# Value packs with zero weights put into a planned TensorE queue of an attention kernel

## The chip, the cores and the metric

The kernel runs on one core of one Trainium2 chip. The metric is device microseconds of one execution, as the median of several. A profile of one more execution gives the rows below; times in them are microseconds from the start of the span unless marked ns. The engines are TensorE (PE, and PEld for its weight loads), VectorE (DVE), ScalarE (ACT), GpSimd (POOL) and SyncE (SP).

## The reference

One input x (1 × 2048 × 512, bf16) goes through two branches with 32 heads of width 16; a sigmoid gate mixes the results per token.

```python
g = sigmoid((x * gate_w).sum(-1, keepdims=True))
# A: softmax attention
scores = einsum("bhqd,bhkd->bhqk", q, k) * 16 ** -0.5
o = einsum("bhqk,bhkd->bhqd", softmax(scores), v)   # then @ A_wo
# B: linear attention with feature maps
phi = concat([softmax(p), softmax(-p)]), p = einsum("bhsd,hdf->bhsf", q or k, w_phi)
o = (phi_q @ (phi_k.T v)) / (phi_q @ phi_k.sum() + 1e-6)   # then @ B_wo
return g * a + (1 - g) * b
```

Branch A has 32 × 2048 × 2048 scores, and an exponential of each.

## The kernel before

**Units and packs.** Branch A is cut into units: the scores of one head, 128 keys (on the partitions) and 512 queries. Four units with the same keys and queries, of four heads, make a pack; there are 512 packs, 16 to a group (16 blocks of 128 keys, `kt` = 0 to 15), and 2048 units.

**Scores.** `_scores` (L663) issues one matmul per unit, which uses 32 of the array's 128 rows; `_qk` issues those of a group of 3 or of 2 units in turn, at different row positions, so that they run beside each other. A group's scores lie in 3 or 2 of a ring of 5 banks of the accumulator memory, so a score group has to wait for the exponential two groups earlier.

**Exponentials.** `_exp` (L702) takes one ACTIVATE on ACT per group, 1536 or 1024 columns: 762 of them for 1905 units. The other 143 units have their exponential made on DVE from integer operations (L597 to L615, from a score matmul named `vqk`).

**Values.** `_pv` queues for each pack one TensorE operation, `_values` (L738): four matmuls (three where DVE makes the fourth unit), each with 128 rows and 32 of the 128 columns of the array, at four column positions side by side; they add into one bank, `ot`, over the 16 key blocks. A unit made on DVE comes as one such matmul by itself (`pvx`). After the last key block `_norm` divides by the sum (L752 to L763).

**The rest.** The projections (`_proj`, L500; values L541), the transposes of x (L478), all of branch B (L836 to L946) and the output projections (L942, L962) are matmuls on the whole 128 × 128 array. They are spread over the span and lie in TensorE's queue between score groups and value packs.

**What sets the order.** Nothing is ordered by hand. `Plan.op` notes each operation with a cost in planned microseconds, its dependencies and a priority; `Plan.order` then plays all engines through, picks at each step the operation that can start first (ties within 0.02 by priority; score groups have priority −1000), and so fixes each engine's queue. `Plan.emit` writes the queues out with the waits on semaphores. Each engine then works its queue strictly in that order. On TensorE a change of `kind` (row for scores, col for values, full) adds `SWITCH` = 0.12 in the plan, and the costs of matmuls in the plan are 0.23 for a score group or a value pack.

Of the kernel before, what the change touches and what calls it, by code (L numbers as in the profile page):

```python
# [10 lines left out]
P = 128  # L11
# [6 lines left out]
F32, BF16 = dt.float32, dt.bfloat16  # L18
# [21 lines left out]
class Op:  # L40
    def __init__(self, eng, fn, cost, name, prio, rel, kind, lat):
        self.eng, self.fn, self.cost, self.name = eng, fn, cost, name
        self.prio, self.rel, self.kind, self.lat = prio, rel, kind, lat
        self.deps = []
        self.users = []
        self.left = 0
        self.need = False
        self.acquire = None
        self.release = None
        self.sem = None  # L50
        self.start = self.end = None
        self.on_commit = None


class Plan:
# [3 lines left out]
    ENGS = ("PE", "ACT", "DVE", "POOL", "SP")  # L59
    LAT = {"PE": 0.20, "ACT": 0.16, "DVE": 0.08, "POOL": 0.12, "SP": 2.2}  # L60
    SWITCH = 0.12

    def __init__(self):
        self.ops = []
# [1 line left out]
        self.free_banks = []  # L66

    def op(self, eng, fn, cost, reads=(), writes=(), deps=(), name="", prio=0.0, rel=-99, kind="full",
           acquire=None, release=None, lat=None):
        o = Op(eng, fn, cost, name, prio, rel, kind, self.LAT[eng] if lat is None else lat)  # L70
        found = {}
        for b in reads:
            for w in b.writers:
                found[id(w)] = w
        for b in writes:
            for w in b.readers or b.writers:
                found[id(w)] = w
            if b.readers:
                for w in b.writers:
                    found[id(w)] = w  # L80
        for d in deps:
            if d is not None:
                found[id(d)] = d
        found.pop(id(o), None)
        o.deps = list(found.values())
        for b in reads:
            b.readers.append(o)
        for b in writes:
            b.writers, b.readers = [o], []
        o.acquire, o.release = acquire, release  # L90
        self.ops.append(o)
        return o

    def order(self):
        avail = {e: [] for e in self.ENGS}
        for o in self.ops:
            o.left = len(o.deps)
            for d in o.deps:
                d.users.append(o)
        for o in self.ops:  # L100
            if not o.left:
                avail[o.eng].append(o)
        free = dict.fromkeys(self.ENGS, 0.0)
        last_kind = None
        queues = {e: [] for e in self.ENGS}
        left = len(self.ops)
        seq = {id(o): i for i, o in enumerate(self.ops)}
        while left:
            best = None
            for e in self.ENGS:  # L110
                for o in avail[e]:
                    if o.rel > self.now:
                        continue
                    t = free[e]
                    for d in o.deps:
                        r = d.end + (d.lat if d.eng != e or e != "PE" else 0.0)
                        if r > t:
                            t = r
                    if o.acquire is not None:
                        if not self.free_banks:  # L120
                            continue
                        r = min(b[1] for b in self.free_banks)
                        if r > t:
                            t = r
                    o.ready = t
                    key = (t, o.prio, seq[id(o)])
                    if best is None or key < best[0]:
                        best = (key, e)
            if best is None:
                low = min((o.rel for e in self.ENGS for o in avail[e] if o.rel > self.now), default=None)  # L130
                assert low is not None, [(o.name, o.eng) for e in self.ENGS for o in avail[e]][:9]
                self.now = low
                continue
            t0, e = best[0][0], best[1]
            pick = None
            for o in avail[e]:
                if o.rel > self.now or (o.acquire is not None and not self.free_banks):
                    continue
                if o.ready <= t0 + 0.02:
                    key = (o.prio, seq[id(o)])  # L140
                    if pick is None or key < pick[0]:
                        pick = (key, o)
            o = pick[1]
            avail[e].remove(o)
            t = max(o.ready, free[e])
            cost = o.cost
            if e == "PE" and o.kind != last_kind:
                cost += self.SWITCH
                last_kind = o.kind
            o.start, o.end = t, t + cost  # L150
            free[e] = o.end
            queues[e].append(o)
            left -= 1
            if o.acquire is not None:
                k = min(range(len(self.free_banks)), key=lambda i: self.free_banks[i][1])
                bank, _, ops = self.free_banks.pop(k)
                o.acquire.bank = bank
                o.deps.extend(ops)
            if o.release is not None:
                self.free_banks.append((o.release.bank, o.end + o.lat, [o]))  # L160
            if o.on_commit:
                o.on_commit(o)
            for u in o.users:
                u.left -= 1
                if not u.left:
                    avail[u.eng].append(u)
        self.queues = queues
        return queues
# [83 lines left out]
class _Kernel:  # L252
# [33 lines left out]
    def _memory(self, ctx):  # L286
# [15 lines left out]
        self.mask = sb("mask", [P, 2], F32)  # L302
        self.bm = sb("bm", [P, 4], F32)
        self.gw = sb("gw", [P, 4], BF16)
        self.gexp = sb("gexp", [P, 2, NT], F32)
        self.gcol = sb("gcol", [P, 2, NT], F32)
        xn_at = at[0]
# [82 lines left out]
    def _consts(self):  # L390
        op = self.plan.op
        B = Buf
# [16 lines left out]
            self.V[:, :, :, 0:136].rearrange("p t c (h v) -> p (t c) h v", v=17)[:, :, :, 16:17], 1.0), 1.0, prio=-70)  # L409
        self.o_vpad = op("POOL", lambda e: e.memset(self.V[:, :, :, 136:], 0.0), 0.5, prio=-69)  # L410
        self.o_vbones = op("POOL", lambda e: e.memset(self.VB[:, :, :, 64:65], 1.0), 0.3, prio=-20)
        self.o_ot = op("DVE", lambda e: e.memset(self.ot, 1.0), 0.6, prio=-60)
        self.b_wphi0 = B()
        z = op("POOL", lambda e: e.memset(self.wphi[:], 0.0), 0.6, prio=-30)
# [165 lines left out]
    def _vector_units(self, g):  # L580
# [11 lines left out]
        for j, u in enumerate(units):  # L592
            job = Job()
            m = op("PE", lambda e, u=u, job=job: self._scores(e, u, self._bank(job)), 0.23,
                   reads=self._score_bufs([u]), name="vqk", prio=due + 2 * j, rel=due + 2 * j - 3, kind="row",
                   acquire=job)
            parts.append(op("DVE", lambda e, j=j, job=job: e.tensor_scalar(  # L597
                vt[:, j, :], self._bank(job), SCALE * LOG2E * 2.0 ** 23, 127.0 * 2 ** 23 + C0 * 2 ** 16,
                op0=ALU.mult, op1=ALU.add), self.c_dve(512), deps=[m] + self.b_vt.readers, name="v_bits",
                prio=due + 2 * j - 40, release=job))  # L600
# [73 lines left out]
    def _qk(self, a, b):  # L674
        plan, NR = self.plan, self.NRING
        units = self.mine[a:b]

        def run(e):
            for k, u in enumerate(units):
                ins = self._scores(e, u, self.ps[:, (a + k) % NR, :])  # L680
            return ins
        k = len(self.qks)
        for x in range(a, b):
            self.in_group[x] = k
        o = plan.op("PE", run, 0.23, reads=self._score_bufs(units), name=f"qk{k}", prio=-1000, kind="row",
                    deps=[self.exps[k - 2]] if k >= 2 else
                    [self.early[x] for x in range(a, b) if x in self.early])

        def commit(_):
            plan.now = max(plan.now, (units[-1] + 1) // 4)  # L690
        o.on_commit = commit
        self.qks.append(o)
# [16 lines left out]
    def _pv(self, p):  # L709
# [9 lines left out]
        if kt == NT - 1:  # L719
            deps += self.late  # L720
            self.late = []
        o = self.plan.op("PE", lambda e: self._values(e, g8, kt, src), 0.23, deps=deps, name=f"pv{p}", prio=p + 2.5,
                         kind="col")
        self.pvs.append(o)
        for u in range(4 * p, 4 * p + 4):
            if u not in self.place:
                tile, made, buf = self.theirs[u]
                x = self.plan.op("PE", lambda e, u=u, tile=tile: self._values(e, g8, kt, {u % 4: tile}), 0.1,
                                 deps=[o] + self.b_V[g8 // 2][kt // 4].writers, reads=[buf], name="pvx", prio=p + 2.6,
                                 kind="col")  # L730
                self.late.append(x)
        if kt == NT - 1:
            self._norm_a(g, o)
# [1 line left out]
    def _values(self, e, g8, kt, src):  # L735
        for i, tile in src.items():
            v0 = 17 * (2 * i + g8 % 2)
            ins = e.matmul(self.ot[32 * i:32 * i + 32, :], self.V[:, kt, g8 // 2, v0:v0 + 32], tile,  # L738
                           start=(kt == 0), stop=(kt == self.NT - 1), tile_position=(0, 32 * i), skip_group_check=True)
        return ins  # L740

    def _norm_a(self, g, last):
        qc, g8 = divmod(g, 8)
# [282 lines left out]
```

## Time and profile before

| | us |
|---|---|
| median of 3 runs | 1002.81 |
| lowest and highest | 1001.78, 1014.02 |
| the profiled execution's own time | 1007.54 |
| its span, from the first to the last instruction | 1005.8 |
| granted TensorE clock, mean over the span | 0.681 of full speed |

The span is what the rows of the profile describe. The granted clock takes two values in it, 1.00 (2.4 GHz) and 0.50 (1.2 GHz). A row of the waits names who waited, at which line, for whom, the total, how many times and the longest. A row of the timeline merges like instructions that follow each other: its start, the time from the first's start to the last's end, engine, line, what is written from what, and the count; a bracket gives idle time of the engine before it and what ended that.

### The profile page before, as it was taken

The page shows a single profiled execution, that of the slowest core. Times are in us where ns is not written, and L with a number is a line of the kernel's source. Part 1 is how long each engine was busy: PE and PEld are TensorE (multiplying, and loading weights), DVE is VectorE, ACT ScalarE, POOL GpSimd, SP SyncE. Part 2 cuts the span into 40 slices and gives each one's busy share as a digit, 9 for nine tenths or more (in the row PEclk, how much of TensorE's full clock was granted, in tenths as well). Part 3 has the DMA queues.
Part 4 walks back from the last instruction along what each step waited for, and adds up shares of the span by engine and source line. Part 5 has one row for each costly group of instructions (what it writes and reads, how often), then busy time and mean ns, then how long its engine had stood idle before and what let it go on. Part 6 is the DMA issues. An engine that isn't in the chain of part 4 may idle for free.

```text
span 1005.8 us, 12680 instructions
## 1 busy us (share of the span) xinstructions
PE 877.1 (87%) x5344; PEld 229.0 (23%) x5344; DVE 735.7 (73%) x1020; ACT 909.6 (90%) x796; POOL 5.2 (1%) x11
## 2 busy tenths in 40 slices
PE   6989898998789879988889998888988898899886
PEld 3333322222121212211112122221221221221111
DVE  3576777658776787766777878888787888787741
ACT  2998999889997999998998989999899999999995
POOL 2000000000000000000000000000000000000000
PEclk9986987559665775855557559675676756855666
DMA  6100000000000000000000000000000000000000
GB/s 210 43 2 1 1 1 2 1 1 1 1 1 1 1 1 1 1 1 1 1 1 1 1 1 11 11 1 1 1 16 6 1 1 1 17 6 1 1 1 22
DMA packets 9737, 9.22 MB, mean 9 GB/s; under 512 B 2512, under 2 KB 9168, under 8 KB 9680
## 3 DMA queue, kind: packets, MB, share of 16 engines
q1 hardware_dynamic: 8624, 7.36, 2.4%
q10 hardware_dynamic: 1056, 1.05, 0.3%
q8 instruction: 42, 0.69, 0.3%
q14 instruction: 15, 0.12, 0.0%
HBM read 6.31 MB, written 2.10 MB: 8 GB/s over the span
## 4 chain that ended last, share of the span: by engine, by line
ACT 52%; PE 43%; DVE 2%; DMA 1%; issue 1%; SPq 0%; DVEq 0%
ACT ET L702 51%; PE ps L663 19%; PE ps L738 11%; PE ps L500 6%; PE ps L942 2%; PE ps L541 1%; ACT bexp L854 1%; PE ps L930 1%; PE ps L836 1%; DVE vt L597 1%; DMA xn<-in_A_x_dram 1%; PE ps L913 1%; PE ps L962 1%; PE ps L876 0%; DVE bsum L856 0%
## 5 line engine op out<-in xcount | busy, mean ns | idle before, releaser
L702 ACT ACTIVATE ET<-ps 128x1536 bf16<-128x1536 f32 x762 | 881.9, 1274 | 82.0 <-PE ps L663 77.9
L663 PE MATMUL ps<-qT,kT 32*128 32x512 bf16 x2048 | 432.5, 521 | 103.1 <-ACT ET L702 98.7
L738 PE MATMUL ps<-ET,V 128*32 128x512 bf16 x1905 | 272.8, 524 | 0.6 <-DVE T L752 0.6
L663 PEld LDWEIGHTS ps<-qT,kT 32*128 32x128 bf16 x2048 | 81.8, 96 | 431.5 <-ACT ET L702 333.9
L597 DVE TENSOR_SCALAR vt<-ps 128x512 uint32<-128x512 f32 x143 | 97.9, 688 | 83.1 <-PE ps L663 82.2
L738 PEld LDWEIGHTS ps<-ET,V 128*32 128x32 bf16 x1905 | 54.2, 99 | 184.7 <-issue 174.5
L615 DVE SCALAR_TENSOR_TENSOR vu<-vt,vu 128x2560 int16<-128x2560 uint32 (+1 forms) x31 | 80.7, 2602 | 0.2
L752 DVE STREAM_TRANSPOSE T<-ps 128x512 f32<-128x512 f32 x64 | 45.3, 709 | 43.0 <-PE ps L738 42.3
L738 PE MATMUL ps<-vu,V 128*32 128x512 bf16 x143 | 75.6, 529 | 0.0
L500 PE MATMUL ps<-xT,WB 128*128 128x512 bf16 x128 | 44.2, 447 | 1.4 <-DVE qT L525 0.7
L500 PE MATMUL ps<-xT,WA 128*128 128x512 bf16 x128 | 44.5, 456 | 0.5 <-DVE vt L597 0.3
L856 DVE TENSOR_REDUCE bsum<-bexp 128x64 f32<-128x1024 bf16 x32 | 38.7, 1211 | 6.2 <-ACT bexp L854 6.0
L605 DVE TENSOR_SCALAR vf<-vt 128x2560 int16<-128x2560 int16 (+1 forms) x31 | 42.7, 1378 | 0.4
L613 DVE TENSOR_TENSOR vu<-vu,vf 128x2560 f16<-128x2560 f16 (+1 forms) x31 | 42.7, 1379 | 0.3
L609 DVE TENSOR_TENSOR vu<-vu,vf 128x2560 f16<-128x2560 f16 (+1 forms) x31 | 42.7, 1378 | 0.3
L861 DVE TENSOR_TENSOR phi<-bexp,brec 128x1024 bf16<-128x1024 bf16 x32 | 39.0, 1218 | 0.3
L854 ACT ACTIVATE bexp<-bsub 128x1024 bf16<-128x1024 bf16 x32 | 34.5, 1080 | 0.0
L815 DVE CAST qkB<-ps 128x512 bf16<-128x512 f32 x32 | 22.0, 687 | 16.6 <-PE ps L500 16.3
L525 DVE TENSOR_SCALAR qT<-ps,mask 128x512 bf16<-128x512 f32 x32 | 23.6, 738 | 12.2 <-PE ps L500 12.0
L842 DVE TENSOR_REDUCE bmx<-ps 128x32 f32<-128x512 f32 x32 | 21.9, 684 | 10.1 <-PE ps L836 10.0
L500 PE MATMUL ps<-WB,xT 128*128 128x512 bf16 x64 | 27.0, 525 | 2.1 <-DVE vt L597 1.8
L541 PE MATMUL ps<-WA,xT 128*128 128x128 bf16 x256 | 26.5, 260 | 0.4 <-DVE vt L597 0.4
(62 smaller groups left out, 508.5 us busy)
## 6 DMA issues: line engine op xcount, KB each, us to landing
xn<-in_A_x_dram SPq DMA_DIRECT2D x4, 512.0 KB, 8.9
out_dram<-outt SPq DMA_DIRECT2D x16, 128.0 KB, 1.7
WB<-in_B_wqkv_dram SPq DMA_DIRECT2D x1, 1536.0 KB, 9.7
WA<-in_A_wqkv_dram ACTq DMA_DIRECT2D x2, 512.0 KB, 7.2
WA<-in_A_wqkv_dram SPq DMA_DIRECT2D x1, 512.0 KB, 9.2
wphi<-in_B_w_phi_dram SPq DMA_DIRECT2D x32, 0.5 KB, 3.4
WoB<-in_B_wo_dram SPq DMA_DIRECT2D x32, 16.0 KB, 1.8
WoA<-in_A_wo_dram SPq DMA_DIRECT2D x1, 512.0 KB, 3.7
```

Of the source, the lines that this page charges most:

```text
L500: ins = e.matmul(self._bank(job)[:, 0:n], lhs(c), rhs(c), start=(c == 0), stop=(c == 3))
L597: parts.append(op("DVE", lambda e, j=j, job=job: e.tensor_scalar(vt[:, j, :], self._bank(job), SCALE * LOG2E * 2.0 ** 23, 127.0 * 2 ** 23 ...
L605: op("DVE", lambda e: e.tensor_scalar(flat(vf), bits, 127, None, op0=ALU.bitwise_and), 0.16 + n * 0.00053, reads=[self.b_vt], writes=[self ...
L609: op("DVE", lambda e: e.tensor_tensor(flat(vu), flat(vu), flat(vf), ALU.mult), 0.16 + n * 0.00053, reads=[self.b_vf, b_vu], writes=[b_vu], ...
L613: op("DVE", lambda e: e.tensor_tensor(flat(vu), flat(vu), flat(vf), ALU.mult), 0.16 + n * 0.00053, reads=[self.b_vf, b_vu], writes=[b_vu], ...
L615: o = op("DVE", lambda e: e.scalar_tensor_tensor(out=flat(vu).bitcast(I16), in0=flat(vt), scalar=2.0 ** -16, in1=flat(vu), op0=ALU.mult, o ...
L663: return e.matmul(out, self.kT[32 * i:32 * i + 32, cp, kt * TOK:(kt + 1) * TOK], self.qT[32 * i:32 * i + 32, s, :], start=True, stop=True, ...
L702: o = plan.op("ACT", lambda e: e.activation(self.ET[:, a % NS:a % NS + n, :], self.ps[:, a % NR:a % NR + n, :], ACT.Exp, scale=SCALE), sel ...
L738: ins = e.matmul(self.ot[32 * i:32 * i + 32, :], self.V[:, kt, g8 // 2, v0:v0 + 32], tile, start=(kt == 0), stop=(kt == self.NT - 1), tile ...
L752: t1 = op("DVE", lambda e: e.transpose(T1.rearrange("p b s -> p (b s)"), src()), 0.74, deps=[last], writes=[b_T1], name="n_t1", prio=due - ...
L854: op("ACT", lambda e: e.activation(ex.rearrange("p s f -> p (s f)"), sub.rearrange("p s f -> p (s f)"), ACT.Exp), self.c_act(1024) + 0.1, ...
L861: op("DVE", lambda e: e.tensor_tensor(self.phi[:, slot].rearrange("p h (s f) -> p s h f", s=2), ex.rearrange("p s (h f) -> p s h f", f=DH) ...
```

## The change

The planner gets a measure of how much of the array the planned TensorE operations use. Each operation has `array`, its cost where nothing else is said, 0.0533 for each unit's matmul in a score group, a value pack, `vqk` or `pvx`. When `order` has picked a TensorE operation, it adds up `array` of the TensorE operations that were planned to start in the last `SPAN` = 3.0 us. A value pack (all but the one with `kt` = 0 of each group) may carry up to two fill packs; as long as the sum is under `SHARE` × `SPAN` = 1.8 us, one is added, for 0.2133 planned us. A fill pack is four matmuls with the shape, column positions and moving tiles of a value pack, whose weights are a tile of zeros, adding into the same bank `ot`; it adds 0 to the result. It stands behind the wait of its value pack and ahead of the pack's own matmuls. The tile of zeros, 128 × 32, is set once on POOL.

```diff
+        self.array = 0.0
+        self.filler = 0
+        self.filled = 0
...
+    SPAN, SHARE, FILL = 3.0, 0.6, 0.2133
...
+        o.array = cost if array is None else array
...
+            if e == "PE":
+                recent = [r for r in recent if r[0] > t - self.SPAN]
+                recent.append((t, o.array))
+                while o.filler > o.filled and sum(r[1] for r in recent) < self.SHARE * self.SPAN:
+                    o.filled += 1
+                    cost += self.FILL
+                    recent.append((t, self.FILL))
             o.start, o.end = t, t + cost
...
+        self.zero = sb("zero", [P, 32], BF16)
...
+        self.b_zero = B()
+        op("POOL", lambda e: e.memset(self.zero[:], 0.0), 0.1, writes=[self.b_zero], prio=-75)
...
-        o = self.plan.op("PE", lambda e: self._values(e, g8, kt, src), 0.23, deps=deps, name=f"pv{p}", prio=p + 2.5,
-                         kind="col")
+        def run(e):
+            for _ in range(o.filled):
+                self._fill(e, src)
+            return self._values(e, g8, kt, src)
+        o = self.plan.op("PE", run, 0.23, reads=[self.b_zero], deps=deps, name=f"pv{p}", prio=p + 2.5, kind="col",
+                         array=0.0533 * len(src))
+        o.filler = 2 if kt else 0
...
+    def _fill(self, e, src):
+
+        for i in range(4):
+            tile = src.get(i, src[0])
+            e.matmul(self.ot[32 * i:32 * i + 32, :], self.zero[:], tile, start=False, stop=False,
+                     tile_position=(0, 32 * i), skip_group_check=True)
```

In the queue as it is built 565 fill packs (2260 matmuls) stand ahead of 326 of the 512 value packs: two ahead of 239, one ahead of 87.

TensorE's queue at a place with little besides scores and values, near 0.50 ms of the span; L663 (after: L679) are the score matmuls, L738 (L760) the value matmuls, `vu` a tile that DVE made, L913 (L942) a transpose of branch B, `zero` the new tile. Before:

```order
L913 MATMUL ps<-iden,phi 128x128 x8
L663 MATMUL ps<-qT,kT 128x512 x3
L738 MATMUL ps<-ET,V 32x512 x4
L663 MATMUL ps<-qT,kT 128x512 x2
L738 MATMUL ps<-ET,V 32x512 x3
L738 MATMUL ps<-vu,V 32x512
L663 MATMUL ps<-qT,kT 128x512 x3
L738 MATMUL ps<-ET,V 32x512 x4
L663 MATMUL ps<-qT,kT 128x512 x6
L738 MATMUL ps<-ET,V 32x512 x4
```

With the change, at the same place:

```order
L942 MATMUL ps<-iden,phi 128x128 x8
L679 MATMUL ps<-qT,kT 128x512 x3
L760 MATMUL ps<-ET,V 32x512 x4
L679 MATMUL ps<-qT,kT 128x512 x6
L768 MATMUL ps<-ET,zero 32x512 x8
L760 MATMUL ps<-ET,V 32x512 x4
L679 MATMUL ps<-qT,kT 128x512 x2
L768 MATMUL ps<-ET,zero 32x512 x8
L760 MATMUL ps<-ET,V 32x512 x3
L760 MATMUL ps<-vu,V 32x512
L679 MATMUL ps<-qT,kT 128x512 x6
L768 MATMUL ps<-ET,zero 32x512 x8
```

Behind the transposes the first value pack has none, and then two fill packs (x8) stand ahead of each value pack; the score group that follows a pack comes behind all three.

TensorE's queue at a place with projections (L500, after L516), near 0.65 ms. Before:

```order
L500 MATMUL ps<-xT,WB 128x512 x2
L663 MATMUL ps<-qT,kT 128x512 x3
L738 MATMUL ps<-ET,V 32x512 x4
L663 MATMUL ps<-qT,kT 128x512
L500 MATMUL ps<-xT,WA 128x512 x4
L663 MATMUL ps<-qT,kT 128x512 x5
L738 MATMUL ps<-ET,V 32x512 x4
L500 MATMUL ps<-xT,WB 128x512 x2
```

With the change:

```order
L679 MATMUL ps<-qT,kT 128x512 x4
L760 MATMUL ps<-ET,V 32x512 x4
L679 MATMUL ps<-qT,kT 128x512
L516 MATMUL ps<-xT,WB 128x512 x4
L679 MATMUL ps<-qT,kT 128x512 x2
L516 MATMUL ps<-xT,WA 128x512 x2
L679 MATMUL ps<-qT,kT 128x512 x3
L768 MATMUL ps<-ET,zero 32x512 x4
L760 MATMUL ps<-ET,V 32x512 x4
L679 MATMUL ps<-qT,kT 128x512 x2
```

Here the value packs among the projections carry no fill pack or one; the projections keep their rough place, in other portions.

## Rows read from the trace of the kernel before

**Rows 1.** The page: busy time by engine, and the granted clock in 40 slices.

```profile
PE 877.1 (87%) x5344; PEld 229.0 (23%) x5344; DVE 735.7 (73%) x1020; ACT 909.6 (90%) x796; POOL 5.2 (1%) x11
...
PEclk9986987559665775855557559675676756855666
```

**Rows 2.** The waits, two rows.

```profile
PE ps L663 <- ACT ET L702: 98.7, 215, 1.5
...
ACT ET L702 <- PE ps L663: 77.9, 95, 16.3
```

**Rows 3.** Timeline of ACT: the first exponentials, some in the middle, the last.

```profile
19.42 5.97 ACT L702 ACTIVATE ET<-ps 128x1536 bf16<-128x1536 f32 x5 [16.29 <-PE ps L663]
...
439.73 4.62 ACT L702 ACTIVATE ET<-ps 128x1536 bf16<-128x1536 f32 x4
445.06 19.94 ACT L702 ACTIVATE ET<-ps 128x1536 bf16<-128x1536 f32 x17 [0.72 <-PE ps L663]
464.85 1.09 ACT L854 ACTIVATE bexp<-bsub 128x1024 bf16<-128x1024 bf16 x1
465.80 4.66 ACT L702 ACTIVATE ET<-ps 128x1024 bf16<-128x1024 f32 x4
...
527.38 2.39 ACT L702 ACTIVATE ET<-ps 128x1536 bf16<-128x1536 f32 x2
...
993.61 1.02 ACT L702 ACTIVATE ET<-ps 128x1024 bf16<-128x1024 f32 x1 [0.92 <-PE ps L663]
```

**Rows 4.** Windows: PE, PEld, DVE, ACT, POOL busy (x); one at 2.4 GHz, sum of 21.

```profile
19.42:69.67 50.25, 44.56 (x370) 16.24 (x368) 31.16 (x46) 50.23 (x45) 0.00 (x0) 1.00 0.10 22
...
sum 336.97, PE 281.33 PEld 88.66 DVE 279.60 ACT 328.98 POOL 0.00; mean PE 13.40 PEld 4.22 DVE 13.31 ACT 15.67 POOL 0.00
```

**Rows 5.** Windows: one of the 21 stretches at 1.2 GHz, and their sum.

```profile
428.07:533.88 105.81, 91.08 (x495) 19.85 (x495) 72.77 (x85) 99.09 (x88) 0.00 (x0) 0.50 0.00 1
...
sum 638.24, PE 581.96 PEld 132.06 DVE 443.84 ACT 579.37 POOL 0.00; mean PE 27.71 PEld 6.29 DVE 21.14 ACT 27.59 POOL 0.00
```

**Rows 6.** Timeline at 1.2 GHz: projections ahead of a score group.

```profile
652.25 1.89 PE L500 MATMUL ps<-xT,WA 128*128 128x512 bf16 x4
...
654.71 2.37 ACT L702 ACTIVATE ET<-ps 128x1024 bf16<-128x1024 f32 x2 [1.98 <-PE ps L663]
```

**Rows 7.** Groups by line and form: the two forms of the exponential.

```profile
L702 ACT ACTIVATE ET<-ps 128x1536 bf16<-128x1536 f32 x381 | 566.6, 1487 | 66.6 <-PE ps L663 64.0
L702 ACT ACTIVATE ET<-ps 128x1024 bf16<-128x1024 f32 x381 | 404.2, 1061 | 15.5 <-PE ps L663 13.9
```

**Rows 8.** Windows, L500 alone: sum at 2.4 GHz, then at 1.2 GHz.

```profile
sum 336.97, PE 59.47 PEld 13.14; mean PE 2.83 PEld 0.63
sum 638.24, PE 51.03 PEld 8.88; mean PE 2.43 PEld 0.42
```

**Rows 9.** Timeline of PE in a stretch at 2.4 GHz.

```profile
421.56 0.39 PE L663 MATMUL ps<-qT,kT 32*128 32x512 bf16 x3
421.88 0.40 PE L738 MATMUL ps<-ET,V 128*32 128x512 bf16 x4
422.21 0.60 PE L500 MATMUL ps<-xT,WA 128*128 128x512 bf16 x2
...
613.93 0.62 PE L738 MATMUL ps<-ET,V 128*32 128x512 bf16 x8
...
614.85 0.62 PE L913 MATMUL ps<-iden,phi 128*128 128x128 bf16 x8
```

**Rows 10.** Timeline of PE in a stretch at 1.2 GHz.

```profile
433.40 1.04 PE L738 MATMUL ps<-ET,V 128*32 128x512 bf16 x8
...
460.54 0.61 PE L663 MATMUL ps<-qT,kT 32*128 32x512 bf16 x3 [0.47 <-ACT ET L702]
461.08 0.62 PE L738 MATMUL ps<-ET,V 128*32 128x512 bf16 x4
461.63 0.61 PE L663 MATMUL ps<-qT,kT 32*128 32x512 bf16 x3
```

More of the change, by code (lines that the diff above doesn't have):

```diff
@@ L68, in op @@
     def op(self, eng, fn, cost, reads=(), writes=(), deps=(), name="", prio=0.0, rel=-99, kind="full",
-           acquire=None, release=None, lat=None):
+           acquire=None, release=None, lat=None, array=None):
         o = Op(eng, fn, cost, name, prio, rel, kind, self.LAT[eng] if lat is None else lat)
@@ L104, in order @@
         last_kind = None
+        recent = []
         queues = {e: [] for e in self.ENGS}
@@ L595, in _vector_units @@
                    reads=self._score_bufs([u]), name="vqk", prio=due + 2 * j, rel=due + 2 * j - 3, kind="row",
-                   acquire=job)
+                   acquire=job, array=0.0533)
             parts.append(op("DVE", lambda e, j=j, job=job: e.tensor_scalar(
@@ L685, in _qk @@
         o = plan.op("PE", run, 0.23, reads=self._score_bufs(units), name=f"qk{k}", prio=-1000, kind="row",
+                    array=0.0533 * (b - a),
                     deps=[self.exps[k - 2]] if k >= 2 else
@@ L729, in _pv @@
                                  deps=[o] + self.b_V[g8 // 2][kt // 4].writers, reads=[buf], name="pvx", prio=p + 2.6,
-                                 kind="col")
+                                 kind="col", array=0.0533)
                 self.late.append(x)
```

## The prediction

> **What bounds the kernel now.** First the page's busy shares [rows 1]: ACT 90%, PE 87%, DVE 73%. Two engines near full, so look at the waits [rows 2]: ACT waited 77.9 us for score matmuls (the longest, 16.3, is the start). PE's 98.7 us of waiting for ACT is the ring of banks. So ACT is the bound, and loses where TensorE is late with scores.
>
> Next, where it loses. The granted clock in the slices [rows 1] moves between 1.00 and 0.50, so I cut the time from the first exponential (19.42) to the end of the last (994.63), 975.2 us [rows 3], at each change of the clock. In the 21 stretches at 2.4 GHz, 336.97 us together, ACT is busy 328.98 us and idle 8.0 (2.4%) [rows 4]. In the 21 at 1.2 GHz, 638.24 us, it is busy 579.37 and idle 58.9 (9.2%) [rows 5]. Nine tenths of the idle time of ACT lie at 1.2 GHz. There the queue stands behind doubled matmuls: four projection matmuls take 1.89 us ahead of a score group, and ACT waits 1.98 us [rows 6].
>
> Idle time is not all. Exponentials that follow each other overlap: four of them take 4.62 us and two take 2.39 [rows 3], so a pair of the two forms costs 2.23 back to back, where their durations add to 1.487 + 1.061 = 2.55 [rows 7]. 381 pairs × 2.23 = 850, plus 32 of branch B at 0.95 (465.80 − 464.85 [rows 3]) = 30: 880 us is what ACT needs. 975.2 − 880 = 95.2 us are lost: 66.9 idle and 28.3 in overlap that a late start gives away. Shared out as the idle time is (88% at 1.2 GHz), the time at 1.2 GHz loses 83.8 us, 13.1% of itself, that at 2.4 GHz 11.4, 3.4%.
>
> What goes with the clock? Not that PE is busy: at 1.2 GHz PE is busy 581.96 of 638.24 us, 91%, in one stretch 91.08 of 105.81 us [rows 5]; at 2.4 GHz 281.33 of 336.97, 83% [rows 4]. What differs is what runs. The projection matmuls L500, which fill the array, take 59.47 us of the time at 2.4 GHz (18%) and 51.03 of that at 1.2 GHz (8%), where each lasts about twice as long [rows 8]. The rest of it holds mostly score groups, on 64 or 96 of 128 rows, in turn with value packs, which use all rows and columns. A fill pack is a value pack but for its weights.
>
> [...] At 1.2 GHz PE is busy 91% [rows 5]. [...]
>
> **The change part by part.**
>
> *The clock.* If the whole time from 19.42 on ran as the stretches at 2.4 GHz did, ACT would need 880 / (1 − 0.034) = 911 us in place of 975.2: −64 us. The bounds are 0 (the clock stays) and −95 (no loss at all).
>
> *The fill packs.* Eight value matmuls take 0.62 us at 2.4 GHz where four take 0.40 [rows 9], so a fill pack costs 0.22; 565 × 0.22 = 124 us of TensorE. It costs nothing where PE would wait for ACT's banks anyway. Check that with the heaviest place: score group, two fill packs, value pack, from one score group to the next: 0.32 + 2 × 0.22 + 0.33 = 1.09 us [rows 9]. At 1.2 GHz the same without fill packs takes 461.63 − 460.54 = 1.09 us [rows 10], so TensorE's load between scores and values becomes what it is now at 1.2 GHz, and no more. Such a pair alone is hidden: from 439.73 to 470.5, nearly all scores and values, ACT idles 0.72 us of 30.7, 2.3% [rows 3]. What loses at 1.2 GHz are the longer jobs between, and these halve, and the planner puts fewer fill packs among them: none or one where projections stand, two elsewhere. The bounds: 0, if all is hidden; and, if the 239 packs with two (47% of 911 us, 428 us) lose as the time at 1.2 GHz does, 428 × (0.131 − 0.034) = +41. Since the nearest row is that of the pairs alone, 2.3% of 428, I take +10.
>
> *What stays at 1.2 GHz.* The first value pack of each group has no fill packs, the plan looks at planned time, and a group of operations without value packs gets none. My estimate, with no row for it, is 45 us still at 1.2 GHz: 45 × (0.131 − 0.034) = +4; bounds 0 and, as a rival, much more.
>
> *The rest.* The tile of zeros is one small POOL instruction at the start, beside the loads. The fill packs stand behind the wait of their value pack, so they add no wait on another engine; behind them in TensorE's queue stand the value pack, the next score group, and the projections, for which DVE waits. DVE's 735.7 us [rows 1] would be 77% of the shorter span, still not the bound. Last, the moved order: score, value and projection work is the same in number. I put these at 0; the 19.4 us ahead and the 11 us behind the exponentials are left as they are.
>
> **Sum**, against the profiled execution's 1007.5: −64 + 10 + 4 = −50, 957.5 us. Its time stands 0.47% above the median of 1002.81, so the forecast in those terms is 957.5 × 0.9953 = 953 us, 5.0% less. About 2% is what a measurement of this kernel can tell from no change.
>
> **Rivals.**
>
> *A. Zero weights do not hold the clock (slower).* What speaks for it: no row shows four column tiles with all weights zero, and if the clock follows what the array's cells do rather than what is issued, zeros may count for little. Against it: transposes, whose weights are an identity and thus nearly all zeros, run inside a stretch at 2.4 GHz (614.85 [rows 9]) that goes on for 20 us behind them. The place is the stretches at 1.2 GHz, the price 0.42 us a pack (1.04 for eight matmuls against 0.62 for four [rows 10]). 565 × 638/975 = 370 packs × 0.42 = 155 us of PE, which is idle only 56 us there [rows 5]: +99 to +155, some +127, or 1130 us. It decides from a point between: with no time at 1.2 GHz the change is worth −54, with all 638 us of it +127, so the lines cross near 190 us, a mean granted clock of about 0.90. Above that the kernel is faster, below it slower.
>
> [...]
>
> *B. The clock rises, and fill packs take the place of doubled matmuls on the way to the scores.* A score group that comes free just after two fill packs began waits 2 × 0.22 + 0.33 = 0.77 us. For it: the queue is strictly in order, and the planner adds the fill packs after it has picked the operation. Against it: the exponential of the other group, 1.06 or 1.49 us [rows 7], runs meanwhile. It gives +41 in place of +10: 988 in the profile's terms, 984 us.
>
> *C. The clock rises for part of the time only*, at the point where A's and the forecast's effects cancel, 190 us at 1.2 GHz: about 1003 us, no change. For it: the plan's time is not the chip's, and fill packs come in lumps. Against it: at 1.2 GHz the same fill packs are there, take longer, and keep the whole array at work until the clock is up again.
>
> **How the numbers follow.** The forecast gets 0.70, B 0.12, A 0.10 (0.04 of it by the rule of the busy engine), C 0.08. The forecast's own range is 930 (fill packs free, nothing at 1.2 GHz, and the 3.4% halved: 880 / 0.983 = 895, +32 = 927 in the profile's terms, rounded up) to 980. The range goes up to 1000, which takes in B and most of C and leaves out A. Faster by over 2% (under 983) holds the forecast and a good half of B: 0.77; within 2%: the rest of B and C, 0.13; slower: A, 0.10.
>
> **What would show it.** Right: a granted clock near 0.95 or more; ACT's share from 90% to about 95%; ACT's waiting for the scores from 77.9 to about 35 us, 16 of it the start; fill packs of 0.22 us each. The clock term is wrong if the slices still show fives in the middle; the term of the fill packs is wrong if the clock is 1.00 and ACT still waits over 60 us, with fill packs ahead of the late score groups; A is right if the clock is as before and PE is busy 95% or more.

## The result, and the profile after

With the change the kernel takes 958.63 us (median of 4 runs, 957.58 to 959.70), where before takes 1002.29 beside it: a ratio of 0.954, 95% interval 0.947 to 0.961. The forecast was 953, the range 930 to 1000. The profiled execution has a span of 956.1 us, 49.7 less than the 1005.8 of before, and a granted clock of 0.941 where it was 0.681.

The page of the change, busy time by engine, the granted clock in 40 slices, and the group of the fill packs (L768, the new matmuls):

```profile
PE 825.8 (86%) x7604; PEld 251.5 (26%) x7604; DVE 729.2 (76%) x1020; ACT 899.4 (94%) x796; POOL 5.4 (1%) x12
...
PEclk9999999999898987978999989999999999999798
...
L768 PE MATMUL ps<-ET,zero 128*32 128x512 bf16 x2260 | 202.2, 417 | 0.0
```

Beside [rows 1]: the fives of the slices are gone, ACT is at 94% where it was at 90, and TensorE, with 2260 matmuls more, is busy for 51 us less. The waits of the change:

```profile
PE ps L679 <- ACT ET L719: 103.3, 219, 1.4
...
ACT ET L719 <- PE ps L679: 43.3, 42, 15.4
```

ACT waited 77.9 us in 95 waits for scores [rows 2]; now 43.3 in 42, of which 15.4 is the start. To see what is left, the time from the first exponential to the end of the last is cut at each change of the clock, as for [rows 4, 5]; full clock is a granted 1.00, half clock a granted 0.50. Columns: the stretch, its length, busy us of PE, PEld, DVE, ACT, POOL, granted clock. First the longest of the 20 stretches at full clock and the sum of them:

```profile
18.54:251.99 233.45, 208.27 (x1924) 69.55 (x1922) 174.16 (x250) 233.45 (x209) 0.00 (x0) 1.00 0.02 6
...
sum 817.70, PE 712.01 PEld 221.07 DVE 653.11 ACT 809.49 POOL 0.00; mean PE 35.60 PEld 11.05 DVE 32.66 ACT 40.47 POOL 0.00
```

Then two of the 19 at half clock and their sum:

```profile
340.74:347.56 6.82, 5.31 (x35) 1.32 (x38) 5.33 (x8) 5.90 (x6) 0.00 (x0) 0.50 0.00 0
...
890.28:903.94 13.66, 13.25 (x87) 2.61 (x87) 8.39 (x21) 10.85 (x10) 0.00 (x0) 0.50 0.01 1
...
sum 109.23, PE 101.47 PEld 23.29 DVE 64.50 ACT 88.60 POOL 0.00; mean PE 5.34 PEld 1.23 DVE 3.39 ACT 4.66 POOL 0.00
```

The time at half clock fell from 638.2 to 109.2 us. At full clock ACT is idle 8.2 of 817.7 us, 1.0% (it was 2.4%); for the first 233 us it never stops. At half clock it is idle 20.6 of 109.2, 19%, where before it was 9.2%. So what is left at half clock is dearer than it was. A piece of the timeline of the change shows one place of it (PE and ACT, at half clock up to 347.56):

```profile
344.97 0.61 PE L679 MATMUL ps<-qT,kT 32*128 32x512 bf16 x2
...
345.51 1.04 PE L768 MATMUL ps<-ET,zero 128*32 128x512 bf16 x8
...
346.33 0.64 PE L760 MATMUL ps<-ET,V 128*32 128x512 bf16 x4
346.76 1.00 PE L768 MATMUL ps<-ET,zero 128*32 128x512 bf16 x8
347.59 0.38 PE L760 MATMUL ps<-ET,V 128*32 128x512 bf16 x3
347.91 0.39 PE L679 MATMUL ps<-qT,kT 32*128 32x512 bf16 x3
...
348.35 1.45 ACT L719 ACTIVATE ET<-ps 128x1536 bf16<-128x1536 f32 x1 [1.71 <-PE ps L679]
```

Two value packs come due together, each behind two fill packs that take 0.82 us now (345.51 to 346.33), and ACT waits 1.71 us for the score group after them (347.91). At full clock the same rows look like this:

```profile
276.56 0.39 PE L679 MATMUL ps<-qT,kT 32*128 32x512 bf16 x3 [0.55 <-ACT ET L719]
276.88 0.61 PE L768 MATMUL ps<-ET,zero 128*32 128x512 bf16 x8
277.32 0.39 PE L760 MATMUL ps<-ET,V 128*32 128x512 bf16 x4
277.65 0.39 PE L679 MATMUL ps<-qT,kT 32*128 32x512 bf16 x2
```

Two fill packs take 277.32 − 276.88 = 0.44 us, 0.22 each, and from score group to score group it is 1.09 us: both as the prediction had them from [rows 9].

### The profile page after: what moved, and what is told of

Its sections match the earlier page's. It is cut to its first block, busy times and chain, and to the rows that moved or that the text cites. A ratio compares the mean times of both kernels' runs of the same rounds, so it can differ in the third digit from the quotient of the medians.

```text
span 956.1 us, 17202 instructions
## 1 busy us (share of the span) xinstructions
PE 825.8 (86%) x7604; PEld 251.5 (26%) x7604; DVE 729.2 (76%) x1020; ACT 899.4 (94%) x796; POOL 5.4 (1%) x12
## 4 chain that ended last, share of the span: by engine, by line
ACT 80%; PE 17%; DVE 1%; DMA 1%; issue 0%; SPq 0%; DVEq 0%
ACT ET L719 77%; PE ps L679 5%; PE ps L768 5%; PE ps L760 3%; ACT bexp L883 3%; DMA xn<-in_A_x_dram 1%; PE ps L971 1%; PE ps L516 1%; PE ps L991 1%; PE ps L942 0%; DVE bsum L885 0%; DVE vt L613 0%; PE ps L959 0%; DMA out_dram<-outt 0%; DVE outt L1003 0%
## 5 line engine op out<-in xcount | busy, mean ns | idle before, releaser
L719 ACT ACTIVATE ET<-ps 128x1536 bf16<-128x1536 f32 x762 | 874.5, 1326 | 44.2 <-PE ps L679 43.3
L679 PE MATMUL ps<-qT,kT 32*128 32x512 bf16 x2048 | 339.9, 402 | 109.5 <-ACT ET L719 103.3
L760 PE MATMUL ps<-ET,V 128*32 128x512 bf16 x1905 | 215.7, 406 | 0.4 <-DVE T L781 0.3
L768 PE MATMUL ps<-ET,zero 128*32 128x512 bf16 x2260 | 202.2, 417 | 0.0
L679 PEld LDWEIGHTS ps<-qT,kT 32*128 32x128 bf16 x2048 | 80.3, 91 | 408.1 <-ACT ET L719 348.0
L760 PEld LDWEIGHTS ps<-ET,V 128*32 128x32 bf16 x1905 | 56.8, 100 | 78.1 <-issue 48.4
L768 PEld LDWEIGHTS ps<-ET,zero 128*32 128x32 bf16 x2260 | 41.0, 96 | 78.5 <-issue 76.1
L760 PE MATMUL ps<-vu,V 128*32 128x512 bf16 x143 | 58.2, 409 | 0.0
L516 PE MATMUL ps<-xT,WA 128*128 128x512 bf16 x128 | 37.9, 397 | 0.5 <-DVE vt L613 0.5
L516 PE MATMUL ps<-xT,WB 128*128 128x512 bf16 x128 | 36.6, 383 | 0.7 <-DVE qT L541 0.4
L788 DVE TENSOR_TENSOR T<-T,rinv 128x256 bf16<-128x256 f32 x64 | 26.5, 415 | 0.6
```

The source lines that it names most:

```text
L516: ins = e.matmul(self._bank(job)[:, 0:n], lhs(c), rhs(c), start=(c == 0), stop=(c == 3))
L679: return e.matmul(out, self.kT[32 * i:32 * i + 32, cp, kt * TOK:(kt + 1) * TOK], self.qT[32 * i:32 * i + 32, s, :], start=True, stop=True, ...
L719: o = plan.op("ACT", lambda e: e.activation(self.ET[:, a % NS:a % NS + n, :], self.ps[:, a % NR:a % NR + n, :], ACT.Exp, scale=SCALE), sel ...
L768: e.matmul(self.ot[32 * i:32 * i + 32, :], self.zero[:], tile, start=False, stop=False, tile_position=(0, 32 * i), skip_group_check=True)
```

## The experiments

All ran beside the kernel before; each ratio is to that kernel's runs on the same chip. The clock is the mean of the profiled execution, and the time at half clock is counted between the first and the last exponential, as above.

| run | median us | ratio, 95% interval | clock | us at half clock | fill packs |
|---|---|---|---|---|---|
| the change, first | 958.63 | 0.954, 0.947 to 0.961 | 0.941 | 109 | 565 |
| the change, again | 959.27 | 0.953, 0.948 to 0.958 | 0.927 | 137 | 565 |
| planned only | 1002.31 | 0.996, 0.993 to 1.000 | 0.683 | 626 | 0 |
| one quarter of a pack | 961.98 | 0.957, 0.953 to 0.962 | 0.919 | 150 | 565 |
| old order | 986.84 | 0.980, 0.974 to 0.985 | 0.913 | 167 | 591 |
| more packs | 965.68 | 0.959, 0.954 to 0.964 | 0.981 | 31 | 1120 |
| a quarter of the rows | 1151.93 | 1.139, 1.127 to 1.151 | 0.668 | 754 | 565 |
| row fill alone | 994.89 | 0.987, 0.981 to 0.994 | 0.708 | 576 | 0 |
| row fill and packs | 946.36 | 0.939, 0.932 to 0.946 | 0.960 | 68 | 565 |
| up to three packs | 943.52 | 0.936, 0.930 to 0.943 | 0.982 | 31 | 697 |
| three packs and row fill | 938.83 | 0.934, 0.929 to 0.939 | 0.986 | 20 | 697 |
| four packs, share 0.55 | 943.73 | 0.938, 0.934 to 0.942 | 0.962 | 65 | 573 |
| value weights | 960.99 | 0.955, 0.950 to 0.960 | 0.927 | 137 | 565 |

**Planned only.** Is it the packs, or the order that the planner lays out for them?

```diff
         def run(e):
-            for _ in range(o.filled):
-                self._fill(e, src)
             return self._values(e, g8, kt, src)
```

> The queue as the change plans it, but the 565 fill packs are not issued; the result is the reference's. Clock theory (the gain is the clock, held up by the fill packs' work): the clock falls back to between 0.65 and 0.75, ACT waits 70 us or more for scores, time within 2% of before, 985 to 1015 us. Order theory (the gain comes from the queue that the planner lays out when it thinks TensorE busier): 955 to 970 us, whatever the clock.

It came out at 1002.31 us and a clock of 0.683. Its clock in the slices and its wait:

```profile
PEclk9996779968557755655557557785576956855565
...
ACT ET L719 <- PE ps L679: 76.3, 99, 14.9
```

That is [rows 2] again, and what the clock theory said. The order theory falls: the new order without the packs is worth nothing that this measurement shows.

**One quarter of a pack.** Does the clock go with how long TensorE is held, or with how much of the array's columns a pack uses?

```diff
-        for i in range(4):
+        for i in range(1):
```

> Each fill pack issues one of its four matmuls, so TensorE is held as long by a pack (0.22 us at 2.4 GHz, 0.42 at 1.2) but with a quarter of the columns; the result is the reference's. Clock theory in the form that the array's work counts: the clock falls to 0.60 to 0.80, and the packs then cost as in rival A, 1010 to 1130 us. [...]

961.98 us, clock 0.919: within its interval the same as the change. The clock theory in the form that the text had (the work of the whole array counts, columns and all) falls here. With one matmul on all 128 rows and 32 columns the clock came out almost as with four side by side (0.941 and 0.927 in the change's two profiles). The fills held TensorE about as long, as the expectation had it; the 565 matmuls are busy for 198.7 us, the 2260 of the change for 202.2:

```profile
L768 PE MATMUL ps<-ET,zero 128*32 128x512 bf16 x565 | 198.7, 424 | 0.3 <-DVE T L781 0.3
```

So of the two that were asked, this run leaves how long TensorE is held.

**A quarter of the rows.** The complement: one matmul a pack, 32 rows and all columns.

```diff
-        for i in range(4):
-            tile = src.get(i, src[0])
-            e.matmul(self.ot[32 * i:32 * i + 32, :], self.zero[:], tile, start=False, stop=False,
-                     tile_position=(0, 32 * i), skip_group_check=True)
+        e.matmul(self.ot[:], self.zero[0:32, :], src[0][0:32, :], start=False, stop=False,
+                 tile_position=(0, 0), skip_group_check=True)
```

> Each fill pack issues one matmul on 32 of the 128 rows and all 128 columns, where one_quarter had one on all rows and 32 columns and kept the clock at 0.92; the result is the reference's. If the clock goes with TensorE being at work, or with columns: clock 0.90 or more, 958 to 975 us. If it goes with the rows that are fed: clock 0.65 to 0.82 and 1000 us or more, since a pack still holds TensorE for 0.4 us there.

1151.93 us, 14% slower than before, at a clock of 0.668, about that of before. The longest stretch at half clock and the sum of all:

```profile
478.33:601.21 122.88, 118.61 (x565) 25.69 (x565) 71.43 (x85) 98.26 (x85) 0.00 (x0) 0.50 0.00 1
...
sum 753.72, PE 732.47 PEld 160.40 DVE 431.59 ACT 568.61 POOL 0.00; mean PE 30.52 PEld 6.68 DVE 17.98 ACT 23.69 POOL 0.00
```

TensorE is busy 732 of 754 us, 97%, at half clock; ACT is idle a quarter of that time. So TensorE can be held nearly all the time with the granted clock at 0.50, busy being read as the profile counts it: a matmul for its whole length, whatever part of the array it uses. Beside the run before it: with a fill on all rows and a quarter of the columns the clock was 0.919, with one on a quarter of the rows and all columns 0.668.

A matmul on a quarter of the rows has the shape of a score matmul, so it could run beside the score group ahead of it and hold TensorE for less. The trace shows both. At full clock:

```profile
603.03 0.39 PE L679 MATMUL ps<-qT,kT 32*128 32x512 bf16 x3
...
603.04 0.39 PE L766 MATMUL ps<-ET,zero 32*128 32x512 bf16 x1
...
603.35 0.40 PE L760 MATMUL ps<-ET,V 128*32 128x512 bf16 x4
...
603.69 0.39 PE L679 MATMUL ps<-qT,kT 32*128 32x512 bf16 x2
...
604.00 0.40 PE L760 MATMUL ps<-ET,V 128*32 128x512 bf16 x3
...
604.97 0.39 PE L679 MATMUL ps<-qT,kT 32*128 32x512 bf16 x3 [0.25 <-ACT ET L719]
...
605.21 0.37 PE L766 MATMUL ps<-ET,zero 32*128 32x512 bf16 x1
...
605.51 0.40 PE L760 MATMUL ps<-ET,V 128*32 128x512 bf16 x4
```

From the score group to the value matmuls it is 0.32 us with a fill beside the group (603.03), 0.31 with none (603.69) and 0.54 with the fill behind it (604.97). Two fill packs between a score group and what follows the value pack, at half clock, first in this run and then in the change:

```profile
499.80 0.61 PE L679 MATMUL ps<-qT,kT 32*128 32x512 bf16 x2
500.20 1.06 PE L766 MATMUL ps<-ET,zero 32*128 32x512 bf16 x2
501.19 0.62 PE L760 MATMUL ps<-ET,V 128*32 128x512 bf16 x4
501.74 0.61 PE L679 MATMUL ps<-qT,kT 32*128 32x512 bf16 x3
```

```profile
283.34 0.61 PE L679 MATMUL ps<-qT,kT 32*128 32x512 bf16 x3 [0.96 <-ACT ET L719]
283.88 1.04 PE L768 MATMUL ps<-ET,zero 128*32 128x512 bf16 x8
284.71 0.64 PE L760 MATMUL ps<-ET,V 128*32 128x512 bf16 x4
285.28 0.61 PE L679 MATMUL ps<-qT,kT 32*128 32x512 bf16 x2
```

It is 1.94 us in both (501.74 − 499.80 and 285.28 − 283.34). So at these places the packs hold TensorE alike, and what differs is the part of the array that they use; how many fills of the run stand beside their score group is not shown. Whether it is the number of rows or that one matmul spans them all is open: no run has a fill on 64 rows. The run shows also what rival A would have cost: packs that hold TensorE while the clock stays down.

**Old order.** The planner lays the packs, but gives them no time, so all queues are those of before with packs put in.

```diff
-                    cost += self.FILL
```

> The fill packs are issued (591 of them), but the planner gives them no time, so that every engine's queue is that of before but for the fill packs. Clock theory: clock 0.90 to 0.96, time 950 to 968 us, since the packs are hidden beside ACT anyway. Rival B (fill packs take ACT's time unless the queue leaves room): clock as high, but ACT waits over 70 us and 975 us or more.

986.84 us, 28 more than the change (ratios 0.980 and 0.954), though the clock is 0.913. The sums at full and at half clock:

```profile
sum 788.22, PE 656.28 PEld 206.14 DVE 628.11 ACT 772.28 POOL 0.00; mean PE 27.35 PEld 8.59 DVE 26.17 ACT 32.18 POOL 0.00
...
sum 167.24, PE 155.31 PEld 37.02 DVE 91.65 ACT 130.69 POOL 0.00; mean PE 6.75 PEld 1.61 DVE 3.98 ACT 5.68 POOL 0.00
```

ACT's idle time at full clock is 15.9 us (2.0%), twice that of the change; at half clock it is 36.6 where the change has 20.6. Both theories missed: the clock is in the first one's range, the time is rival B's, and ACT's 66.4 us of waiting for scores is just under rival B's 70. So rival B is right of a queue that leaves no room for the packs. The order that is worth nothing without them is worth 28 us with them; part of that may be the packs themselves, 26 more here and at other places.

**More packs, up to three packs.** What do packs cost where the clock is up already?

```diff
-    SPAN, SHARE, FILL = 3.0, 0.6, 0.2133
+    SPAN, SHARE, FILL = 3.0, 0.75, 0.2133
-        o.filler = 2 if kt else 0
+        o.filler = 3 if p else 0
```

> Share 0.75 in place of 0.6, up to three fill packs on every value pack but the first: 1120 in place of 565. What is left with the change is 109 us at 1.2 GHz, in which ACT idles 23 of its 29 us. Clock theory: the clock goes to 0.98 or more, ACT waits about 25 us (15 of it the start), 935 to 950 us. Rival B (TensorE gets too full: 555 packs more are 122 us of it): clock 0.98 or more, but 960 us or more, with ACT waiting for scores at 2.4 GHz.

The other has the last line alone, with the share of 0.6:

> The change with up to three fill packs on any value pack but the first, at the same planned share of 0.6. If the low stretches that are left come from the limit of two and the first key block: clock 0.96 or more and 945 to 956 us. If more packs cost as much as they give (as with 1120 packs): clock 0.96 or more, 957 to 968 us.

Their sums at full clock, the run with 1120 packs first:

```profile
sum 904.72, PE 848.31 PEld 282.66 DVE 699.52 ACT 882.32 POOL 0.00; mean PE 121.19 PEld 40.38 DVE 99.93 ACT 126.05 POOL 0.00
```

```profile
sum 879.57, PE 781.97 PEld 245.86 DVE 697.18 ACT 872.80 POOL 0.00; mean PE 97.75 PEld 30.73 DVE 87.15 ACT 109.10 POOL 0.00
```

Both are at half clock for 30.7 us, so the clock is the same; what differs is 423 packs, and the order that the planner lays out round them: 22 us more (ratios 0.959 and 0.936, with intervals that do not meet), 0.05 us a pack. ACT idles 22.4 us at full clock in the one and 6.8 in the other. With 1120 packs rival B's clock, time and waits are there; with 697 they are not, and the 132 packs more than in the change go with 15 us less. The expectation of the run with three packs holds for its first theory, just below its range; it changes the limit and the first key block together, and they were not taken apart. (The 23 us at half clock in the first expectation are 20.6 by the sums above.)

**Four packs, share 0.55.** As many packs as the change, at other places.

```diff
-    SPAN, SHARE, FILL = 3.0, 0.6, 0.2133
+    SPAN, SHARE, FILL = 3.0, 0.55, 0.2133
-        o.filler = 2 if kt else 0
+        o.filler = 4 if p else 0
```

> Up to four fill packs, at a planned share of 0.55: 573 packs, as many as the change has (565), but laid where the plan is emptiest. If where the packs stand decides and not how many: clock 0.97 or more and 940 to 952 us. If their number decides: clock near 0.94 and 953 to 962 us.

943.73 us with 573 packs, against 959.27 of the change beside it with 565. At the same number, where the packs stand decides; the limit, the share and the first key block were changed together, and which of them did it is open. The packs stand in larger lumps than the change's, ahead of 271 value packs in place of 326, and the time at half clock is 65 us. The clock (0.962) is a little under what was expected of it.

**Row fill, alone and with packs.** If rows are what goes with the clock, a score group on two or three quarters of the rows can take one more matmul with zero weights on a free quarter, beside its own; a fill beside a score group took no time of its own at 603.03 above (0.32 us, where 0.31 is without one). It is left out where the bank `ot` is not in the middle of a sum and where the group before has one on another quarter.

```diff
+            self._row_fill(e, k, units)
             for j, u in enumerate(units):
...
+    def _row_fill(self, e, k, units):
+        free = [x for x in range(4) if x not in {u % 4 for u in units}]
+        if k - 1 in self.rows:
+            free = [x for x in free if x == self.rows[k - 1]]
+        if not self.open or not free:
+            return
+        i = self.rows[k] = free[0]
+        s = self._unit(units[0])[4]
+        e.matmul(self.ot[:], self.zero[32 * i:32 * i + 32, :], self.qT[32 * i:32 * i + 32, s, :], start=False,
+                 stop=False, tile_position=(32 * i, 0), skip_group_check=True)
```

> No fill packs; instead 359 score groups get one more matmul with zero weights on a free quarter of the rows, beside the group's own, adding 0 into ot; the queue is otherwise that of the change without packs (as planned with array shares and no fill: that of before). Rows theory: clock 0.75 to 0.88 at no TensorE time, 970 to 992 us. Rival (whole passes count, or columns): clock 0.66 to 0.72 and 992 to 1010 us.

> The change with the row fills of e6 added in 353 score groups. Rows theory: clock 0.96 or more, ACT waits for scores under 38 us, 944 to 955 us. Rival (the extra matmul makes the score group late): 960 us or more at any clock.

> Up to three fill packs on any value pack but the first (697 packs), and the row fills beside score groups. If the two effects add: clock 0.985 or more, 934 to 943 us. If three packs have already taken what the clock can give: 940 to 950 us, the same as cap3 within its interval.

Alone it is worth little: 994.89 us, clock 0.708, inside the rival's ranges and not in those of the rows theory. The time at half clock is 576 us against 638 of before, whose queue it has [rows 5]. An estimate of the size: the rows that the 359 matmuls fed are a sixth of what the 565 of one quarter of a pack fed (359 × 32 against 565 × 128), and the fall of 62 us is an eighth of the 488 there. So the run does not speak against the rows, but the expectation had its effect too large. Together with the change the row fill is worth 13 us, and the rows theory holds in all three of its numbers: clock 0.960, 946.36 us, ACT waiting 33.1 us for scores. The time at half clock is 68 us where the change's two profiles have 109 and 137; the ratio's interval (0.932 to 0.946) lies below that of the change run again (0.948 to 0.958). On top of three packs it gives 938.83, the fastest of all and in the range of its first theory, but its interval does not part it from three packs alone.

**Value weights.** Do zeros count for less?

```diff
-            e.matmul(self.ot[32 * i:32 * i + 32, :], self.zero[:], tile, start=False, stop=False,
+            e.matmul(self.ot[32 * i:32 * i + 32, :], self.V[:, 0, 0, 0:32], tile, start=False, stop=False,
```

> The change with weights from the values of the first key block in place of zeros, so that each fill pack adds terms to the sums that the reference does not have. If zero weights are to the clock what others are: within 1% of the change, clock 0.93 to 0.95. If the clock looks at what the cells add up: a higher clock, 0.97 or more, and under 950 us.

> The change itself once more, beside the others on one chip: 950 to 962 us, clock 0.93 to 0.95.

960.99 us at a clock of 0.927, against 959.27 at 0.927 for the change beside it: in this kernel these weights made no difference to the clock. That answers the doubt behind rival A.

## Why the prediction was right, and where its terms were not

*What bounds the kernel* held: ACT is the bound, its losses lay at half clock, and with the clock up the kernel gained nearly what was worked out: 975.2 us from the first exponential to the end of the last became 926.9, −48.3 where the sum said −50.

*The terms* did not come out one by one; two errors of about 20 us cancelled, which is luck. What ACT loses at each clock can be counted in the traces, exponential by exponential: the time from the start of one to the start of the next, less the 1.331, 0.904 or 0.947 us that this takes where they follow without a wait (1536 columns, 1024, branch B; 882 us for all). By this count before loses 11.5 us (3.4%) at full clock and 81.8 (12.8%) at half, which bears out the prediction's shares. The change loses 17.7 us (2.2%) and 27.1 (25%).

- *The clock and the fill packs.* The prediction took 3.4% lost at full clock and 10 us for the packs, −64 + 10 = −54. At the measured 2.2%, all the time at full clock would be 882 / 0.978 = 902 us, −73. So with the packs in it, the time at full clock loses less than it did without them. That the packs are hidden where the planner makes room, and that the doubled jobs of neighbouring stretches, whose backlog the 3.4% held, are gone, is argued from the sums; no run takes it apart.
- *What stays at half clock.* This is the term that was mis-sized: it had 45 us at the price of before, +4. It was 109 us, and each lost 25% where 13% was taken: 109 × (0.248 − 0.022) = +25. At the place shown above the loss is the doubled fill packs ahead of a score group. That this is the price throughout is not shown: the low stretches lose 25 to 28% in the change, one quarter of a pack, old order and four packs, and 12.7% in the run that is planned only, but the stretches that are left may also be the heavier ones. What can be had there is shown by the two runs with a limit of three and of four, which have 31 and 65 us at half clock and are 15 us faster, the second with hardly more packs than the change.

*Rival A* did not come: with zero weights the clock was that with values (0.927). Packs that hold TensorE but not the clock (0.668) cost 1152 us, where it said 1130. Its line between faster and slower, 190 us at half clock, was not met exactly by any run; the nearest has 167 us and is 2% faster.

*Rival B* did not come with the change, but is real: with the queues of before the packs cost 28 us more, and with 1120 packs 22 us more than with 697.

*The rule of the busy engine*, with 0.04 of rival A's chance, is a term that no run shows; what they showed is TensorE busy for 91% of the time at half clock and 83% at full clock before [rows 4, 5], and for 97% at half clock with a quarter of the rows. What the prediction read from the trace, that value packs use all rows and all columns, was half of it: with a quarter of the columns (clock 0.919) the time was the same within the interval, with a quarter of the rows (0.668) the gain was gone.

*What would show it* came near: clock 0.941 for 0.95, ACT 94% for 95, waits 43.3 us for 35, packs of 0.22 us as said.

## What to carry to other kernels

Where the engine that bounds a kernel idles mainly while TensorE is at half clock, cut the profile at each change of the clock and compare what that engine loses on both sides: the difference is what a higher clock can give, here 64 of 1007 us foreseen for the clock alone and 50 got in all. Empty matmuls bought that clock here, those on all rows (0.941, and 0.919 with one a pack) and not one a pack on a quarter of them (0.668), and they are paid for in the queue: let whatever orders the queue count their time, try other places for the same number of them, and stop when the clock is up. Look then at the low stretches that are left, since two fill packs took 0.83 us there (283.88 to 284.71) and 0.44 elsewhere (276.88 to 277.32).

## What the runs showed of the hardware

- One matmul a pack on 128 rows and 32 columns kept the granted clock at 0.919; one on 32 rows and 128 columns left it at 0.668, with TensorE busy 97% of its 754 us at half clock. The 565 matmuls of the first kind were busy for 198.7 us, the 2260 of the whole packs for 202.2; with two fills of the second kind it was 1.94 us from a score group to what follows the value pack, at one place at half clock, as with two whole packs.
- Weights of zero and weights of data gave the same clock, 0.927, and the same time within the interval, 959.27 and 960.99 us.
- A matmul with zero weights on rows that a score group leaves free lowered the time at half clock from 109 or 137 us to 68 beside the fill packs.
